# Output stores issued from SP instead of from ACT in a fused windowed-attention and feed-forward kernel

## The chip, the cores and the metric

The kernel runs on one core of one Trainium2 chip. The metric is the device time of one execution in microseconds (us); the time given is the median of 5 runs. A second source is one profiled execution, from which all durations below are read.

## The reference

For 8 batches of 8 heads with 576 positions of 64 values the kernel computes attention in a window of 32 positions to each side, puts the heads side by side into a matrix x of 4608 tokens by 512, and feeds it through two matrix products with a leaky ReLU between them:

```python
scores = q @ k.T / 8                      # per batch and head
scores = where(|i - j| <= 32, scores, -1e9)
attn   = softmax(scores)
x      = (attn @ v) as [B * S, H * D]     # 4608 x 512
h      = x @ w_in                         # 512 -> 2048
out    = maximum(0.01 * h, h) @ w_out     # 2048 -> 512
```

Inputs and output are float32; the kernel computes its products in bfloat16 with float32 sums.

## The kernel before

Work is staged in units that an outer program written by hand interleaves.

*Attention.* The heads are taken in 4 pairs a batch and the 576 queries in 2 halves, so there are 64 steps. Step i needs the score (`score`): five small matmuls into the PSUM tile `ps` (there is one such buffer), an exponential on ACT into `e` (L248), and on GpSimd (POOL) the product with the window mask into `pr` (L252). Then `weighted` has the row sums `s` (L274, or L276 and L279) and the weighted values `x` (L286) on PE, and a reciprocal (L292) and a product into `xT` (L294) on VectorE (DVE). Scores run one or two steps ahead of `weighted`.

*Inputs.* `load_qk` and `load_v` bring q, k and v of one batch and one pair into float32 tiles `qf`, `kf` and `vf` (L72 and L83; v in two halves). There is one buffer for each of the four pairs, so the load of the next batch can start only once the casts to bfloat16 have read the buffer: `cast_qk` (L168, on POOL, in the opening on DVE too) into `qb` and `kb`, and `cast_v` (L178) into `vbd`. q and k have to be transposed: for the first three batches PE does it (L201), from batch 3 on DMA transposes do (L187), issued once the cast is done. ACT copies the transposed q and k into `qT` and `kT` (L209, L215), and DVE places the keys into `kbd` (L227).

*Feed-forward.* `h_tile` computes one 128 x 288 tile of h (four matmuls, L305) and ACT applies the leaky ReLU (L309). `o_tile` computes 128 tokens of the output: 16 matmuls of 512 columns (L322), a copy from PSUM into `o_sb` by ACT (L327), and a store to the output in DRAM (L328). There are 36 such tiles; the last is cut into two parts of 384 and 128 columns, so there are 37 stores. `o_sb` has four buffers.

*Order.* Nothing is reordered by a scheduler; each engine works through its instructions in the order in which the program writes them. A list `plan` holds the h and o tiles, and `spend` (called before each h tile and, as the hook, four times inside each o tile) puts an attention step between them when its due time has come. So a step's casts, loads and DMA transposes are written in the middle of an o tile's matmuls, and a tile's store after them.

*Queues.* The engine SP issues all loads of q, k and v and all DMA transposes, and does nothing else. POOL issues the loads of the two weight matrices, all in the first 32 us. ACT issues the stores, between its activations. A DMA instruction waits in its engine's queue until its semaphores are there: for a store, the copy of its `o_sb`; for a load, the casts that read its buffer. Besides, in the built program the DMAs of SP and ACT together share eight completion counters, and each DMA waits until the previous one on its counter is done, whichever engine issued that.

Of the kernel before, what the change touches and what calls it, by code (L numbers as in the profile page):

```python
# [16 lines left out]
def kernel(  # L17
# [12 lines left out]
    nc = tc.nc  # L30
# [107 lines left out]
    for lo in (0, 64):  # L138
        w = win[lo:lo + 64]
        nc.gpsimd.affine_select(  # L140
            out=w, in_=w, compare_op=ALU.is_ge, fill=0.0,
# [3 lines left out]
            out=w, in_=w, compare_op=ALU.is_ge, fill=0.0,  # L145
# [167 lines left out]
    def o_tile(j, hook=None):  # L313


        cols = (0, 512) if j < NTOK // 128 - 1 else (0, 384, 512)
        for lo, hi in zip(cols[:-1], cols[1:]):
            o = mmps.tile([128, 512], FP32, name="mm", tag="mm")
            for f in range(FFC):
                if hook and lo == 0 and f % 4 == 0:  # L320
                    hook()
                nc.tensor.matmul(  # L322
                    o[:, lo:hi], gT[:, f, ds(128 * j % RING, 128)], w_out_bf[:, f, lo:hi],
                    start=(f == 0), stop=(f == FFC - 1),
                )
            o_sb = outp.tile([128, DMODEL], FP32, name="o_sb")
            nc.scalar.activation(out=o_sb[:, lo:hi], in_=o[:, lo:hi], func=AF.Copy)  # L327
            nc.scalar.dma_start(out=out[ts(j, 128), lo:hi], in_=o_sb[:, lo:hi])  # L328

    def keep_busy(n):  # L330

# [204 lines left out]
    for us, kind, g, f in plan:  # L536
        if kind == "h":
            spend(us)
            h_tile(g, f)
        elif f == 0:  # L540
            o_tile(g, lambda: spend(O_US))
# [28 lines left out]
```

## Time and profile before

| what | value |
|---|---|
| median of 5 runs | 328.82 us (327.81 to 329.25) |
| profiled execution: its own time | 328.82 us |
| profiled execution: span, first to last instruction | 327.1 us |
| PE busy | 306.7 us, 94% of the span |
| DVE, ACT, POOL busy | 226.3 us (69%), 223.3 us (68%), 180.5 us (55%) |
| SP's DMA queue q1 | 34.22 MB, packets' time 55.4% of 16 DMA engines |
| ACT's DMA queue q10 (the stores) | 9.44 MB, 8.3% |
| POOL's DMA queue q0 (the weights) | 4.20 MB, 7.7% |
| issue of one store on ACT | 0.34 us, 37 times |

How to read it: times on a timeline count from the start of the span. PE is the matmuls, PEld the weight loads beside them; ACT, DVE and POOL are the other compute engines; a q behind an engine's name (SPq, ACTq) marks an instruction by which its queue issues a DMA. Such an instruction does not count as busy, nor does waiting for a semaphore. In a list of waits each row says who waited for whom, the total in us, how often, and the longest. PEclk is the share of TensorE's full clock that was granted.

By stretches of the span PE is busy for 9.15 of the first 20 us, 17.32 of the next 20, 9.90 of the 10 to 50 us, 13.52 of the 16 to 66 us and 23.84 of the 24 to 90 us; from 90 to 306 us it is busy for 214.9 of 216 us. The first store is issued at 56.75 us, the last at 324.53 us.

### The profile page before, as it was taken

The numbers are of one execution on the slowest core, as the hardware profiler recorded it, in microseconds if no ns is written. First come the engines' busy times: TensorE is split into PE (matmuls) and PEld (weight loads), VectorE is DVE, ScalarE is ACT, GpSimd is POOL, SyncE is SP. The second block draws the span as 40 slices with busy tenths as digits, with TensorE's granted clock in tenths as the row PEclk, the third lists the DMA queues.
The fourth block names the chain that finished last, engine by engine and source line by source line (L and its number), as shares of the span: only waits on it lengthen the run. The fifth ranks groups of instructions, "written<-read, shape, count | busy, mean of one in ns | idle before, by whom it ended". The sixth has DMA issues, their size and how long they took to land.

```text
span 327.1 us, 6571 instructions
## 1 busy us (share of the span) xinstructions
PE 306.7 (94%) x2463; PEld 205.7 (63%) x2485; DVE 226.3 (69%) x310; ACT 223.3 (68%) x432; POOL 180.5 (55%) x213
## 2 busy tenths in 40 slices
PE   2578999799999999999999999999999999999996
PEld 1346784367585665757575766667675767676653
DVE  5489743579874997779777988688858867565200
ACT  5784792249385898878787888878786646465541
POOL 7699748647774696519741597339642545131000
PEclk9999999899999999999999999999999999999999
DMA  8999979968999999945995199916831001010102
GB/s 182 212 201 217 270 192 202 238 166 195 233 181 214 208 209 240 203 127 121 207 230 129 69 181 249 210 66 95 181 82 65 34 17 50 0 66 0 67 13 84
DMA packets 85172, 48.28 MB, mean 148 GB/s; under 512 B 64020, under 2 KB 80660, under 8 KB 85140
## 3 DMA queue, kind: packets, MB, share of 16 engines
q1 hardware_dynamic: 75524, 34.22, 55.4%
q10 hardware_dynamic: 5328, 9.44, 8.3%
q0 software_dynamic: 4288, 4.20, 7.7%
q8 instruction: 19, 0.31, 0.4%
q14 instruction: 13, 0.11, 0.1%
HBM read 36.70 MB, written 9.44 MB: 141 GB/s over the span
## 4 chain that ended last, share of the span: by engine, by line
PE 80%; DMA 9%; DVE 3%; SPq 3%; POOL 2%; issue 1%; ACT 0%; ACTq 0%; DVEq 0%
PE mm L322 35%; PE mm L305 34%; DMA kf<-in_k_dram 9%; PE ps L242 4%; PE x L286 4%; DVE r L292 2%; PE s L274 2%; SPq L72 2%; SPq L83 1%; POOL vbd L484 1%; PE tp L201 1%; DVE xT L294 1%; POOL kb L168 1%; POOL pr L252 1%; PE mm L335 0%
## 5 line engine op out<-in xcount | busy, mean ns | idle before, releaser
L292 DVE RECIPROCAL r<-s 128x288 f32<-128x288 f32 x64 | 125.1, 1954 | 34.5 <-PE s L274 25.1
L252 POOL TENSOR_TENSOR pr<-e,mask 128x544 bf16<-128x544 bf16 x64 | 78.0, 1218 | 101.8 <-ACT e L248 81.9
L305 PE MATMUL mm<-xT,w_in_bf 128*128 128x288 bf16 x1024 | 133.1, 286 | 0.0
L322 PE MATMUL mm<-w_out_bf,gT 128*128 128x512 bf16 (+2 forms) x571 | 129.9, 376 | 1.1
L309 ACT ACTIVATE gT<-mm 128x288 bf16<-128x288 f32 x256 | 101.0, 414 | 21.1 <-PE mm L305 8.6
L305 PEld LDWEIGHTS <-w_in_bf 128*128 128x128 bf16 x1024 | 98.3, 98 | 23.9
L322 PEld LDWEIGHTS <-gT 128*128 128x128 bf16 x592 | 56.8, 99 | 60.7 <-issue 1.7
L248 ACT ACTIVATE e<-ps 128x544 bf16<-128x544 f32 x64 | 40.0, 624 | 25.9 <-PE ps L242 6.0
L327 ACT ACTIVATE o_sb<-mm 128x512 f32<-128x512 f32 (+2 forms) x37 | 21.7, 586 | 47.0 <-PE mm L322 47.0
L227 DVE COPY kbd<-kT 64x576 bf16<-64x576 bf16 x64 | 28.6, 447 | 29.2 <-ACT kT L215 28.7
L178 POOL CAST vbd<-vf 64x576 bf16<-64x576 f32 x58 | 38.7, 668 | 2.2 <-DMA vf<-in_v_dram 0.3
L294 DVE TENSOR_TENSOR xT<-x,r 128x288 bf16<-128x288 f32 x64 | 29.3, 458 | 6.7
L168 POOL CAST kb<-kf 96x768 bf16<-96x768 f32 x32 | 27.4, 857 | 10.1 <-DMA kf<-in_k_dram 10.1
L242 PE MATMUL ps<-qT,kbd 128*128 128x128 bf16 (+2 forms) x320 | 26.8, 216 | 2.1 <-ACT e L248 2.1
L286 PE MATMUL x<-pr,vbd 128*128 128x128 bf16 (+2 forms) x320 | 26.4, 215 | 1.4 <-DVE xT L294 0.9
L242 PEld LDWEIGHTS <-kbd 128*128 128x128 bf16 x320 | 20.9, 101 | 10.6 <-issue 2.8
L263 DVE TENSOR_TENSOR both<-pr 128x256 bf16<-128x256 bf16 x52 | 23.0, 441 | 3.6 <-POOL pr L252 2.5
L209 ACT ACTIVATE qT<-qT 128x576 bf16<-128x576 bf16 x20 | 23.6, 1179 | 1.2 <-ACT o_sb L327 1.2
L286 PEld LDWEIGHTS <-vbd 128*128 128x128 bf16 x320 | 21.0, 99 | 4.9 <-issue 1.6
L215 ACT ACTIVATE kT<-kT 128x576 bf16<-128x576 bf16 x20 | 23.6, 1179 | 0.0
L265 DVE COPY both<-pr 128x32 bf16<-128x32 bf16 x52 | 21.7, 417 | 0.0
L168 POOL CAST qb<-qf 96x768 bf16<-96x768 f32 x24 | 19.7, 822 | 0.0
(39 smaller groups left out, 110.3 us busy)
## 6 DMA issues: line engine op xcount, KB each, us to landing
qf<-in_q_dram SPq DMA_DIRECT2D x32, 288.0 KB, 4.7
kf<-in_k_dram SPq DMA_DIRECT2D x32, 288.0 KB, 5.4
vf<-in_v_dram SPq DMA_DIRECT2D x64, 144.0 KB, 5.3
out_dram<-o_sb ACTq DMA_DIRECT2D x35, 256.0 KB, 2.1
w_in_bf<-in_moe_w_in_dram POOLq DMA_DIRECT2D x8, 256.0 KB, 6.8
w_out_bf<-in_moe_w_out_dram POOLq DMA_DIRECT2D x4, 512.0 KB, 14.0
qT<-qb SPq DMA_TRANSPOSE x20, 4.9
kT<-kb SPq DMA_TRANSPOSE x20, 4.0
```

The source lines that it names most:

```text
L168: eng.tensor_copy(out=dst[:, p], in_=src[b, p].rearrange("p a (c d) -> p c a d", d=D),)
L178: nc.gpsimd.tensor_copy(out=vbd[b % 2][r, p, :, r], in_=vf[b, p][r])
L227: nc.vector.tensor_copy(out=kbd[b % 2][r, p, :, r], in_=kT[r].rearrange("p (n j) -> p n j", j=64),)
L242: nc.tensor.matmul(ps[:, c0:c0 + n], kbd[b % 2][:, p, blk], qT[b][:, p, q0:q0 + n], start=True, stop=True,)
L248: nc.scalar.activation(out=e, in_=ps[:, 512 - HALF:512 - HALF + NCOL], func=AF.Exp, scale=scale,)
L252: nc.gpsimd.tensor_mul(pr, e, mask[hf])
L286: nc.tensor.matmul(x[:, a:a + n], vbd[b % 2][:, p, blk, :], pr[:, c0:c0 + n], start=(n_ == 0), stop=(n_ == len(WIN[hf]) - 1), skip_group_c ...
L292: nc.vector.reciprocal(r, s)
L294: nc.vector.tensor_mul(xT[:, p, t0:t0 + HALF], x, r)
L305: nc.tensor.matmul(h[:, 0:HALF], w_in_bf[:, c, ts(f, 128)], xT[:, c, ds(t0, HALF)], start=(c == 0), stop=(c == DMC - 1),)
L309: nc.scalar.activation(out=gT[:, f, ds(t0, HALF)], in_=h[:, 0:HALF], func=AF.Prelu, alpha=0.01,)
L322: nc.tensor.matmul(o[:, lo:hi], gT[:, f, ds(128 * j % RING, 128)], w_out_bf[:, f, lo:hi], start=(f == 0), stop=(f == FFC - 1),)
```

## The change

The store of `o_tile` is issued from SP (`nc.sync`) instead of from ACT (`nc.scalar`). Nothing else is edited:

```diff
             o_sb = outp.tile([128, DMODEL], FP32, name="o_sb")
             nc.scalar.activation(out=o_sb[:, lo:hi], in_=o[:, lo:hi], func=AF.Copy)
-            nc.scalar.dma_start(out=out[ts(j, 128), lo:hi], in_=o_sb[:, lo:hi])
+            nc.sync.dma_start(out=out[ts(j, 128), lo:hi], in_=o_sb[:, lo:hi])
```

In the built program PE, DVE and POOL keep their instructions and their order. ACT loses the 37 stores. SP gets them at the places where the program writes them: the first before the load of `qf` of batch 2 and pair 0, the second before `qf` of pair 1, and so on; those from 248 us on come after all loads and transposes. Which of the eight counters a DMA uses changes with this for nearly all DMAs after the first store.

## The prediction

> **What bounds the kernel now.** I read the page first (busy shares, then the chain that ended last), then the waits of PE and of ACT, then the stretch from 50 to 70 us in small windows and as a timeline. PE is busy for 94% of the span and holds 80% of the chain, so the question is where PE loses time at all. The list of PE's waits for the whole span has one entry of size once the opening is over, and ACT's list has its cause:
>
> ```profile
> PE ps L242 <- ACT e L248: 2.1, 1, 2.1
> ...
> ACT e L248 <- DMA vf<-in_v_dram: 4.0, 1, 4.0
> ACT e L248 <- DMA kf<-in_k_dram: 3.6, 1, 3.6
> ```
>
> The columns are total us, times, longest. An exponential reads PSUM and needs no DMA, yet ACT sat before two of them until a load landed. From 70 us to the end PE's waits sum to only 0.3 us. The chain, in order of time (start, us, what), shows what stood between:
>
> ```profile
> 54.52 6.91 DMA kf<-in_k_dram
> ...
> 61.50 0.34 ACTq L328
> ...
> 61.94 0.64 ACT e L248
> ...
> 62.62 0.40 PE ps L242 x5
> ```
>
> The second output store stood in ACT's queue until that load landed, although its data was ready at 57.74 + 0.59 = 58.33. In the built program each DMA of SP or ACT counts on one of eight completion counters and waits until that counter's previous DMA is done; the second store got the counter of this kf load (issued 54.52), the first store that of the last vf load before it (issued about 51.0). The timeline of ACT has both holds:
>
> ```profile
> 57.22 0.62 ACT L248 ACTIVATE e<-ps 128x544 bf16<-128x544 f32 x1 [4.04 <-DMA vf<-in_v_dram]
> ...
> 61.94 0.62 ACT L248 ACTIVATE e<-ps 128x544 bf16<-128x544 f32 x1 [3.60 <-DMA kf<-in_k_dram]
> ```
>
> PE pays twice, as windows of 2 us show (length, then PE busy; PEclk is the number ahead of the last two):
>
> ```profile
> 60.00:62.00 2.00, 0.54 (x3) 0.14 (x2) 1.03 (x2) 0.06 (x1) 0.54 (x1) 1.00 1.15 227
> 62.00:64.00 2.00, 1.38 (x14) 1.06 (x14) 0.71 (x1) 1.19 (x2) 1.29 (x2) 0.80 1.13 234
> 64.00:66.00 2.00, 2.00 (x7) 0.60 (x6) 1.70 (x2) 0.60 (x1) 1.86 (x3) 0.50 1.13 247
> ```
>
> First it is idle for 2.1 us, then it runs at half clock. PE's timeline prices the second part:
>
> ```profile
> 63.43 3.46 PE L322 MATMUL mm<-w_out_bf,gT 128*128 128x512 bf16 x8
> ```
>
> The next score matmul starts at 66.73, so eight of these took 3.30 us where the full pace (16 in 3.45 us on the chain, for example from 141.64) is 0.216 us each, 1.73 us.
>
> [...]
>
> **The change part by part.**
> (a) Removed from ACT: 37 issues of 0.34 us, 12.6 us, with their counter waits. From 70 us on this is worth nothing on the path: PE waits 0.3 us there and ACT has room (58.8 of 72 us busy in 162 to 234). The cover is PE's own work, and ACT stays shorter than PE.
> (b) Removed: the two holds. Without the first, ACT does the score of 57.22 about 3.5 us earlier; without the second, that of 61.94 can follow its matmuls (58.34) at once. PE's wait goes: **-2.0 us** (2.1 less a usual hop). With no such hole the half clock goes too: 3.30 - 1.73 = **-1.6 us**. What could be late next is POOL's mask product, the DVE chain, or a vbd cast: POOL is busy 10.6 of 16 us in 52 to 68, so 3.6 us less leaves it 10.6 of 12.4. I allow **+0.2 us** for a new small gap there (today's wait of x for a cast is 0.4).
> (c) Added to SP: the same 37 issues, 12.6 us, each waiting for its o_sb from ACT. SP has room on average (it stands 48.3 us at L187 waiting for POOL's kb), but it takes turns, so I went through its new order. In 53 to 66 us the first store comes just before the load of qf of batch 2; its data is there at 52.59 + 0.60 = 53.2, so that load goes 0.5 us late. The second comes before qf1, kf1, qf2 and kf2 (now 54.02 to 55.50) and its data comes only near 57.9 (nine of its sixteen matmuls run from 55.35 on at 0.216 us, then the copy of 0.59): those four go 3.9 us late, the vf halves behind them 4 to 5 us, qf3 and kf3 (59.03, 60.20) 5 to 6 us. In these is that the first vf half now waits for the first store's counter (53.3 plus a landing of 7.4, so 60.7). Who waits: the batch 2 casts. kf3, the tightest, lands near 60.20 + 7.9 = 68.1 (7.9 is the kf median from issue to landing in 50 to 70 us) and is first read by POOL at 82.77, 14.7 us later; less 6 us for the delay and 3.5 us for the earlier reader, 5 us remain. Cost 0, covered by that slack. After 100 us, stores stand ahead of DMA transposes: stores issued now at 106.79, 110.85, 145.76, 183.52, 217.82, 234.97, transposes behind them at 109.95, 114.21, 148.91, 186.66, 220.96, 238.73. The store is ready 3.1 to 3.8 us before the transpose may start, since that waits for a POOL cast: cost 0.
> (d) The other way round, stores wait behind SP's loads and transposes (a transpose issues in 1.2 us and more). With four o_sb buffers and a store every 3.4 to 13 us a store may be some 10 us late before ACT waits for a buffer: cost 0, and it has no effect below nothing.
> (e) Stores and loads on one ring. The bytes are the same; q10's share is 8.3% of 16 engines. Nearest row: a store lands in 7.4 us among loads, 2.1 us in quiet. Bounds: from 0.5 us gained[...] to 5 us lost (rival 3). I take 0.
> (f) The tail: the last store needs a hop from ACT to SP, as the gaps of 0.05 to 0.1 us between SP's instructions suggest: +0.1 us. ACT no longer issues (0.34) between the last two copies, but the second waits for PE, so nothing comes back.
> Sum: -2.0 - 1.6 + 0.2 + 0.1 = **-3.3 us**. The profiled execution took 328.82 us (span 327.1 plus 1.7), which is also the median of the runs shown, so 325.5.
>
> **Rivals.** (1) *The gain is halved by POOL.* POOL is full from 50.3 to 56.5 (memsets, two products, four casts), and its products feed PE. If it is late by 1.5 to 2 us in place of ACT and PE's clock still drops for a while: 327.2. For it: with 10.6 us of work in 12.4 us POOL has little room. Against: from 56.5 POOL waits for ACT 1.50 us and then 2.17 us.
> (2) *Nothing moves.* The holds on ACT return as holds of the loads, and PE waits for loads instead: 328.8. Against: the slack of 5 us in (c), and that the two stores' new counters belong to vf loads issued near 47 and 48 us.
> (3) *Slower: the shared ring makes transposes late.* Four keys are near their use: kT issued at 187.98, 193.52, 222.27 and 226.54, with the median landing of 4.0 us, are read by ACT (L215) at 193.91, 198.66, 228.20 and 232.97, so 1.1 to 2.4 us spare. If landings on the one ring grew by 4 us, batch 6 would lose 4 - 1.1 = 2.9 and batch 7 4 - 1.9 = 2.1 us, 5 us in all: 330.5. It decides from about 3.2 us of growth, where the two overruns reach 3.3. Against: stores near those transposes are issued 3 us earlier and land in about 2 us. The extreme is a tenth of that chance, some 335.
>
> **How the numbers follow.** Forecast (-3.3, with 324.5 to 326.6 for its own spread: 1 us for the clock, 0.5 for a run): 0.72. Rival 1: 0.11. Rival 2: 0.06. Rival 3: 0.11. The bound of what a measurement tells from no change is 0.3%, 1 us. Faster is forecast and most of rival 1: 0.82; within it rival 2 and a rest: 0.07; slower rival 3: 0.11. The range goes from 324.0 to 327.9: it leaves out rival 3, part of rival 2 and little below.
>
> **What would show it.** Right: the two DMA entries are gone from ACT's waits; 60 to 66 us has PE full and PEclk 1.00; SP shows L328, with the qf and kf loads behind the second store near 58 us; PE's waits after 70 us stay under 1 us; span near 323.8. Wrong in (b): PEclk still falls near 60 us, or PE waits for POOL. Wrong in (c): POOL's or DVE's casts of batch 2 wait for DMA near 70 to 85 us. Wrong in (e): ACT waits at L209 or L215 for a DMA and PE waits after 100 us.

## The result and the profile after

The changed kernel takes 327.42 us (median of 28 runs, 326.05 to 328.61) where the kernel before takes 328.63 us (median of 49). The ratio is 0.9961, with a 95% interval of 0.9950 to 0.9973: 1.2 us faster, where 3.3 us were forecast.

The part near 60 us went as forecast. The page's PEclk row shows nines throughout; windows of 2 us (length, PE busy, ..., PEclk third from the end) of the profile after show it in place:

```profile
60.00:62.00 2.00, 1.85 (x15) 0.95 (x13) 2.00 (x2) 0.89 (x2) 1.86 (x3) 1.00 1.06 253
62.00:64.00 2.00, 2.00 (x20) 1.23 (x19) 1.90 (x5) 0.95 (x2) 0.70 (x2) 1.00 1.14 237
64.00:66.00 2.00, 1.95 (x14) 1.05 (x14) 1.77 (x4) 0.08 (x1) 0.81 (x1) 1.00 1.26 231
```

PE is busy 5.8 of these 6 us at full clock (before: 3.9, much of it at half). (Among PE's busy times given ahead of the prediction, 9.90 us belong to 40 to 50 us, 13.52 us to 50 to 66 us and 23.84 us to 66 to 90 us.) ACT's waits in 50 to 66 us name no DMA any more:

```profile
ACT o_sb L327 <- PE mm L322: 7.3, 4, 2.4
ACT e L248 <- PE ps L242: 3.8, 3, 1.8
ACT e L248 <- POOL vbd L178: 0.6, 1, 0.6
```

SP's timeline (start, length, instruction) shows the new order, with the four loads of q and k held by the second store until 57.15:

```profile
53.04 0.58 SPq L328 DMA_DIRECT2D out_dram<-o_sb  x1
53.72 0.37 SPq L72 DMA_DIRECT2D qf<-in_q_dram  x1
54.19 0.42 SPq L72 DMA_DIRECT2D kf<-in_k_dram  x1
57.15 0.36 SPq L328 DMA_DIRECT2D out_dram<-o_sb  x1
57.60 0.39 SPq L72 DMA_DIRECT2D qf<-in_q_dram  x1
```

What was not forecast stands in PE's waits from 70 us to the end, which summed to 0.3 us before:

```profile
PE s L274 <- DVE r L292: 1.0, 1, 1.0
PE x L286 <- DVE xT L294: 0.6, 2, 0.3
```

A good yardstick is the start of ACT's copy of an output tile (L327), because a tile's copy follows PE's progress. From tile to tile, in us, with the medians of the two kernels:

| kernel | median | start to tile 0 | tile 0 to 4 | 4 to 11 | 11 to the last copy | last copy to end |
|---|---|---|---|---|---|---|
| before | 328.63 | 52.59 | 31.94 | 56.55 | 183.14 | 2.90 |
| after | 327.42 | 52.05 | 28.17 | 58.32 | 183.12 | 3.40 |
| difference | -1.2 | -0.54 | -3.77 | +1.77 | -0.02 | +0.50 |

The first column is chance: no instruction differs there, and it ran from 52.05 to 54.38 us over the profiles of this study. Without it the profiles differ by 1.5 us, about what the medians do. So 3.8 us were gained, and 1.8 us were given back between tiles 4 and 11 and 0.5 us at the end.

Where the 1.8 us went: of the profile before, the timelines of DVE and of POOL near 125 us.

```profile
125.28 0.29 DVE L263 TENSOR_TENSOR both<-pr 128x256 bf16<-128x256 bf16 x1
125.49 0.17 DVE L265 COPY both<-pr 128x32 bf16<-128x32 bf16 x1
125.57 1.95 DVE L292 RECIPROCAL r<-s 128x288 f32<-128x288 f32 x1
```
```profile
126.03 1.22 POOL L252 TENSOR_TENSOR pr<-e,mask 128x544 bf16<-128x544 bf16 x1 [1.47 <-issue]
```

The same two, and PE, of the profile after, at the same step (24, the first of batch 3):

```profile
120.97 0.29 DVE L263 TENSOR_TENSOR both<-pr 128x256 bf16<-128x256 bf16 x1
121.18 1.19 DVE L265 COPY both<-pr 128x32 bf16<-128x32 bf16 x1
122.29 1.95 DVE L292 RECIPROCAL r<-s 128x288 f32<-128x288 f32 x1
```
```profile
121.12 1.22 POOL L252 TENSOR_TENSOR pr<-e,mask 128x544 bf16<-128x544 bf16 x1 [1.47 <-issue]
```
```profile
124.29 0.28 PE L274 MATMUL s<-both,ones_bd 128*128 128x288 bf16 x1 [1.03 <-DVE r L292]
```

DVE copies 32 columns. Before, it was through 0.4 us ahead of POOL's product; after, the product starts 0.06 us ahead of the copy, and the copy ends 0.03 us after the product does, so it takes 1.19 us. The reciprocal behind it is 1 us late, and PE, which needs the single buffer `s` back, waits 1.03 us. The next step collides too, there with POOL's casts of q and k:

```profile
125.64 0.79 DVE L263 TENSOR_TENSOR both<-pr 128x256 bf16<-128x256 bf16 x1
126.35 0.80 DVE L265 COPY both<-pr 128x32 bf16<-128x32 bf16 x1
```
```profile
125.46 0.82 POOL L168 CAST qb<-qf 96x768 bf16<-96x768 f32 x1
126.23 0.89 POOL L168 CAST kb<-kf 96x768 bf16<-96x768 f32 x1
```

Why they meet now: ACT's timeline after the copy of tile 9, before and after.

```profile
124.18 0.61 ACT L327 ACTIVATE o_sb<-mm 128x512 f32<-128x512 f32 x1
124.82 0.34 ACTq L328 DMA_DIRECT2D out_dram<-o_sb  x1
125.27 0.62 ACT L248 ACTIVATE e<-ps 128x544 bf16<-128x544 f32 x1 [0.48 <-ACT o_sb L327]
```
```profile
119.89 0.59 ACT L327 ACTIVATE o_sb<-mm 128x512 f32<-128x512 f32 x1
120.37 0.62 ACT L248 ACTIVATE e<-ps 128x544 bf16<-128x544 f32 x1
```

The exponential followed the copy's start by 1.09 us and now follows it by 0.48 us, so POOL's product comes 0.6 us sooner after it. DVE's copy does not (1.31 and 1.29 us after the start of ACT's copy). The store issue on ACT had been keeping the two apart.

### The profile page after: what moved, and what is told of

Read it like the earlier page. It is cut to its first block, busy times and chain, and to the rows that moved or that the text cites. A ratio compares the mean times of both kernels' runs of the same rounds, so it can differ in the third digit from the quotient of the medians.

```text
span 325.1 us, 6587 instructions
## 1 busy us (share of the span) xinstructions
PE 305.2 (94%) x2463; PEld 205.2 (63%) x2485; DVE 224.6 (69%) x310; ACT 224.7 (69%) x432; POOL 180.3 (55%) x213
## 3 DMA queue, kind: packets, MB, share of 16 engines
q1 hardware_dynamic: 80852, 43.66, 63.6%
## 4 chain that ended last, share of the span: by engine, by line
PE 77%; DMA 7%; DVE 6%; POOL 3%; SPq 2%; ACT 2%; issue 2%; DVEq 0%; POOLq 0%; ACTq 0%
PE mm L322 34%; PE mm L305 32%; DMA kf<-in_k_dram 7%; PE x L286 4%; PE ps L242 4%; DVE r L292 4%; PE s L274 2%; SPq L72 1%; SPq L83 1%; POOL vbd L484 1%; DVE xT L294 1%; PE tp L201 1%; POOL kb L168 1%; ACT kT L215 1%; POOL vbd L178 1%
## 5 line engine op out<-in xcount | busy, mean ns | idle before, releaser
L322 PE MATMUL mm<-w_out_bf,gT 128*128 128x512 bf16 (+2 forms) x571 | 128.3, 373 | 1.1
L309 ACT ACTIVATE gT<-mm 128x288 bf16<-128x288 f32 x256 | 104.4, 413 | 25.2 <-PE mm L305 9.6
L327 ACT ACTIVATE o_sb<-mm 128x512 f32<-128x512 f32 (+2 forms) x37 | 21.7, 586 | 55.8 <-PE mm L322 55.8
L227 DVE COPY kbd<-kT 64x576 bf16<-64x576 bf16 x64 | 28.5, 446 | 24.8 <-ACT kT L215 24.2
L265 DVE COPY both<-pr 128x32 bf16<-128x32 bf16 x52 | 22.7, 437 | 0.0
L263 DVE TENSOR_TENSOR both<-pr 128x256 bf16<-128x256 bf16 x52 | 21.2, 408 | 0.5
```

The source lines that it names most:

```text
L227: nc.vector.tensor_copy(out=kbd[b % 2][r, p, :, r], in_=kT[r].rearrange("p (n j) -> p n j", j=64),)
L309: nc.scalar.activation(out=gT[:, f, ds(t0, HALF)], in_=h[:, 0:HALF], func=AF.Prelu, alpha=0.01,)
L322: nc.tensor.matmul(o[:, lo:hi], gT[:, f, ds(128 * j % RING, 128)], w_out_bf[:, f, lo:hi], start=(f == 0), stop=(f == FFC - 1),)
```

## The experiments

Theory A is this collision. Theory B is that the moved stores make loads or transposes late on SP or in its queue q1, where the page of the profile after has the stores too (43.66 MB, no q10; the prediction and an expectation call that queue a ring). Kernels of one group share the runs of the kernel before. Ratios are to that kernel, with the 95% interval.

**First group** (before: 328.92 us).

All stores from SP, the changed kernel again.

> The changed kernel again, beside its variants. Theory A (a collision gives the gain back): PE gains 3.5 to 4 us between 50 and 66 us; near 121 us the DVE copy L265 runs while POOL's product L252 runs and takes 1.2 us in place of 0.17, PE waits for the reciprocal about 1 us there and 1.5 us in all, and about 0.5 us goes at the end; so 1.2 to 2 us faster than before. Theory B (the moved stores make transposes or loads late): the same total, but ACT or POOL wait for a DMA after 100 us.

327.89 us, ratio 0.9965 (0.9950 to 0.9981). Its profile repeats the pattern: 28.08 us from tile 0 to 4, 58.31 us from 4 to 11, 3.40 us at the end. No wait of ACT or PE for a DMA appears after 100 us. POOL's list there puts two waits of its mask product, 3.8 us in all, down to a DMA; in the kernel before it has four, 6.8 us in all, so Theory B's sign is absent.

The first four stores alone from SP:

```diff
-            nc.sync.dma_start(out=out[ts(j, 128), lo:hi], in_=o_sb[:, lo:hi])
+            (nc.sync if j < 4 else nc.scalar).dma_start(out=out[ts(j, 128), lo:hi], in_=o_sb[:, lo:hi])
```

> The stores of tiles 0 to 3 from SP, all others from ACT as before. Theory A: the holds at 53 to 61 us are gone, ACT keeps its 0.34 us issue near 120 us so POOL's product comes after the DVE copies, and the tail is that of before: 3.3 to 3.8 us faster than before, 325.0 +- 0.5. Theory B would also give this, since no store stands among transposes. If the gain near 60 us is itself smaller than 3.5 us, this one shows only 1 to 2 us.

325.37 us, ratio 0.9909 (0.9876 to 0.9943), so 3.6 us faster. 28.33, 56.55 and 2.91 us in the same three places: the gain is kept and nothing is given back. The forecast's size was right for this part.

All from SP but tile 9 (`j != 9`):

> All stores from SP except that of tile 9 (the copy at about 119.9 us), which ACT issues. Theory A: the exponential behind it comes about 0.45 us later, POOL's product starts after the DVE copies, L265 near 121 us takes 0.17 us, and 1.2 to 1.7 us come back against all_sp (about 326). Theory B: one store in 37 changes nothing on a ring, so the same time as all_sp within 0.3 us.

326.39 us, ratio 0.9918 (0.9892 to 0.9944). Against all_sp 1.5 us come back in the medians (0.5 of them at the end, which takes 2.91 us here). Between tiles 4 and 11 it takes 57.34 us, 1.0 us less than all_sp and 0.8 us more than before. L265 of step 24 is down to 0.17 us, and one collision is left, in the next step, as DVE's timeline shows:

```profile
126.29 1.19 DVE L265 COPY both<-pr 128x32 bf16<-128x32 bf16 x1
```

All from SP, step 24 not joined:

```diff
-        if JOINED - 1 <= i < NC - 1:
+        if JOINED - 1 <= i < NC - 1 and i + 1 != 24:
```

> All stores from SP; step 24 alone is not joined: its two DVE instructions L263 and L265 are gone and PE makes the row sums from the two parts of pr with two matmuls (L276, L279; 0.1 us more), the result being the same sum. Theory A: the collision near 121 us has no DVE copy to hit, PE's wait for the reciprocal goes, 1.0 to 1.6 us come back against all_sp. Theory B: no change, within 0.3 us.

326.85 us, ratio 0.9938 (0.9914 to 0.9962), 1.0 us better than all_sp by the medians; the two intervals overlap a little, so the profile has to carry this. Its stretch from tile 4 to 11 takes 57.56 us, 0.8 us less than all_sp. Here too the collision moved on by one step, and PE's waits still have it:

```profile
PE s L274 <- DVE r L292: 0.7, 1, 0.7
```

Theory B expected no change from either kernel; in the profiles one store alone moves 1.0 us of this stretch, and one join alone 0.8 us.

**Second group** (before: 328.64 us).

The kernel before, with tiles 9 and 10 alone from SP (`j in (9, 10)`):

> The kernel before, with the stores of tiles 9 and 10 alone moved to SP. Theory A (freeing ACT of the 0.34 us issue in that place lets POOL's product meet the DVE copies): slower than before, by 1.0 to 1.8 us, about 330.3; L265 near 125.5 us takes 1.2 us and PE waits for the reciprocal there, while the hole at 60 us and the half clock stay. Theory B (what was lost is a matter of SP's queue as a whole): two stores more on SP change nothing, within 0.3 us of before.

330.75 us, ratio 1.0067 (1.0041 to 1.0093): slower by 2.1 us, with the interval from 1.3 to 3.1. The stretch from tile 4 to 11 takes 58.31 us, as in all_sp: two of the 37 stores carry its whole loss. DVE's and POOL's timelines:

```profile
125.49 1.21 DVE L265 COPY both<-pr 128x32 bf16<-128x32 bf16 x1
```
```profile
125.45 1.22 POOL L252 TENSOR_TENSOR pr<-e,mask 128x544 bf16<-128x544 bf16 x1 [0.88 <-POOL vbd L178]
```

and PE's waits, the old hole of 60 us (`ps`) among them:

```profile
PE s L274 <- DVE r L292: 1.8, 2, 1.0
PE ps L242 <- ACT e L248: 1.7, 1, 1.7
PE x L286 <- DVE xT L294: 1.0, 4, 0.3
```

Of these, one wait for the reciprocal (1.0 us) and two for `xT` (0.6 us) are near 128 to 134 us. The others belong to the hole, and there an expectation missed: the half clock did not stay. PEclk is 1.00 throughout, and PE's timeline has the same eight matmuls at full pace, but then a wait that the profile before does not have:

```profile
62.58 0.40 PE L242 MATMUL ps<-qT,kbd 128*128 128x64 bf16 x5 [1.74 <-ACT e L248]
63.29 1.89 PE L322 MATMUL mm<-w_out_bf,gT 128*128 128x512 bf16 x8
69.83 0.28 PE L274 MATMUL s<-both,ones_bd 128*128 128x288 bf16 x1 [0.78 <-DVE r L292]
```

From tile 0 to 4 it takes 31.35 us, hardly less than the 31.94 us before.

The kernel before, with tile 1 alone from SP (`j == 1`):

> The kernel before, with the second store alone (tile 1, the one that stood for the kf load until 61.50 us) moved to SP. If that hold alone made PE's hole and the half clock: all of first4_sp's gain, 3.3 to 3.8 us, about 325.4, with ACT still held near 57 us. If the first hold matters as much: about half.

324.98 us, ratio 0.9898 (0.9867 to 0.9929), 3.7 us faster: one store has the whole gain. One expectation missed: ACT is not held near 57 us by the first store either, which it issues at once, as its timeline shows.

```profile
53.51 0.38 ACTq L328 DMA_DIRECT2D out_dram<-o_sb  x1
54.91 0.62 ACT L248 ACTIVATE e<-ps 128x544 bf16<-128x544 f32 x1 [1.43 <-PE ps L242]
```

Moving the second store changed the counters of its neighbours too. So this kernel takes away both holds, and the weight of each alone isn't settled by it.

All from SP but tiles 9 and 10 (`j not in (9, 10)`):

> All stores from SP except tiles 9 and 10, which ACT issues. Theory A: j9_act had one collision left (L265 of the next step, 1.19 us at 126.3 us, with 0.8 us of PE lost); with the second store on ACT too, L265 takes 0.17 us in both steps and 0.5 to 0.9 us more come back: 325.6 to 326.0, within 0.5 us of first4_sp. Theory B: as all_sp, near 327.8.

324.85 us, ratio 0.9888 (0.9863 to 0.9913), the fastest by its median, 3.8 us faster than before and 0.8 us below the expected range. The stretch takes 56.56 us, 0.8 us less than j9_act, as expected; the medians differ by 1.5 us, more than the profiles explain. In step 24 the copy is through before the product starts, in DVE's and POOL's timelines:

```profile
122.07 0.17 DVE L265 COPY both<-pr 128x32 bf16<-128x32 bf16 x1
```
```profile
122.84 1.21 POOL L252 TENSOR_TENSOR pr<-e,mask 128x544 bf16<-128x544 bf16 x1 [2.29 <-issue]
```

With 35 of 37 stores on SP, Theory B has nothing left to explain.

All from SP but the last two tiles (SP for `j < 34`; with the last tile's two parts these are three stores, not the four of the expectation):

> All stores from SP except the last four (tiles 34 and 35), which ACT issues: 0.3 to 0.5 us faster than all_sp if the longer time from the last copy to the end of the span (3.1 us in all_sp's profile, 2.6 in first4_sp's) belongs to SP's issue; no difference if it is a matter of chance in the landing. The collisions near 121 us stay, so about 327.4 at best.

326.96 us, ratio 0.9955 (0.9933 to 0.9976), against 0.9965 for all_sp: the intervals overlap, so the times are inconclusive. In the profile the end takes 2.92 us in place of 3.40 (the expectation counts it from the end of the last copy, the table from its start).

**Third group** (before: 328.92 us).

All from SP, steps 24 and 25 not joined (`i + 1 not in (24, 25)`):

> All stores from SP, steps 24 and 25 not joined (the DVE instructions L263 and L265 of both are gone, PE makes the row sums from the two parts of pr: 0.1 us more a step, the same sum). Theory A (collisions of DVE copies with POOL's product): with no copy left to hit in the two steps, the time from tile 4's to tile 11's copy is back at 56.6 to 56.9 us (58.3 with the collisions), and the kernel is 2.7 to 3.5 us faster than before. If the issue on ACT mattered in another way than through the collision, the 58.3 us stay.

325.51 us, ratio 0.9898 (0.9866 to 0.9930), 3.4 us faster; the stretch takes 56.38 us. ACT is as free as in the changed kernel, POOL's products come as early, and with no DVE copy to hit in these steps the loss is gone. By itself this edit also takes 0.46 us of undisturbed DVE work from each of the two steps; but j9_10_act keeps both joins, undisturbed, and its stretch is as short (56.56 us). Together they show that it was the collision, not the freed ACT in another way.

Tiles 0 to 3 from ACT, the others from SP (`j >= 4`):

> The counterpart of first4_sp: tiles 0 to 3 stored from ACT, all others from SP. If the change is the sum of two parts (a gain of some 3.6 us in the first four stores, a loss of some 2.1 us in tiles 9 and 10 and 0 to 0.5 us at the end), this is 1.8 to 2.6 us slower than before, about 331.

330.40 us, ratio 1.0049 (1.0034 to 1.0063): slower by 1.5 us, a little less than expected. 31.42 and 58.32 us: almost no gain, the full loss of 1.8 us, but an end of 2.92 us. Here too the hole is there (1.49 us) and PEclk stays at 1.00. The end's 0.5 us that I had counted as part of the loss isn't there.

## Why the prediction fell short, step by step

**Reading what bounds the kernel** was right: ACT's holds made PE's hole, and after the opening no other loss of PE of that size was there to be had. That the half clock follows from the hole was an estimate from one profile, and does not hold for the others (see (b)).

**(b), the holds:** right in its sum, with 3.6 us less 0.2 forecast and 3.77 us measured, but partly by luck. The half clock was priced at 1.6 us on top of the hole. In the profiles of only9_10_sp and rest_sp the hole is there without it, and tile 0 to 4 still takes 31.35 and 31.42 us, 3.2 to 3.3 us more than in the changed kernel: its matmuls run at full pace, and PE then waits 0.8 us for a reciprocal and 0.4 us for `xT`. So the hole with what follows it costs 3.2 us or so at full clock, and the half clock only 0.5 to 0.6 us more. The runs of the kernel before in the three groups agree: 46 of 75 had a mean clock of 0.998 or more (the profiled one, with 3.4 us at half, has 0.995) and a median of 328.57 us, the other 29 one of 329.20 us. In the profile before, PE was busy for 1.95 of the 2 us from 58 to 60, then idle for 2.08 us at a stretch, and the drop came after that (PEclk 0.50 in 64 to 66 us). The idle stretches of 1.74 us in only9_10_sp and of 1.49 us in rest_sp were followed by none. How long an idle stretch has to be, and whether its length alone decides, these three profiles do not show.

POOL, feared as the next to be late, kept up (PE's one wait in 48 to 70 us of the profile after is 0.2 us, for `xT`), so rival 1's mechanism did not come in that stretch. That its number, 327.2, is close to the time measured is chance.

**(c), SP's new order:** right. The second store was issued at 57.15 (57.9 forecast) and the four loads behind it at 57.60 to 59.10; no cast of batch 2 waited for DMA, and the transposes were not late. Rival 2 falls with it.

**(d), (e), stores and loads in one queue:** right at 0. In the profile after, the stores' bytes are in SP's queue (q1 has 43.66 MB, and there is no q10). A store landed in 2.2 us (2.1 before), qf and kf in 4.4 and 5.2 us (4.7 and 5.4), transposes in 4.4 and 3.6 us (4.9 and 4.0). Rival 3 asked for transposes 3 us later; it did not come.

**(a), ACT's freed issue, is the step that failed.** It said that from 70 us on this "is worth nothing on the path", because PE hides ACT there. It cost 1.8 us, through a chain that the step did not follow: a faster ACT gives POOL its product sooner, the product now starts ahead of a DVE copy and holds it (1.19 us in place of 0.17), and PE's only buffer for the row sums comes back late. PE's waits after 70 us, which were to stay under 1 us, came to 1.6 us. The sum used busy shares and PE's waits of before; both say how much room there is on average, not which instructions will now run at once. I had asked what is late next only in 50 to 68 us, where time was gained, not wherever an issue was removed. The material was in the profile before: the page gives L265 a mean of 417 ns, while by itself it takes 0.16 to 0.17 us. Of the 52 copies, the 26 that overlap no work of POOL took 0.161 to 0.170 us, and 20 of the other 26 took 0.64 to 1.19 us. That an overlap with POOL costs a DVE copy time, and how much, is read from these durations; what the two engines contend for, they do not tell.

**(f), the end:** forecast at +0.1, measured at +0.5 us. The traces place it: the last store lands 2.42 us after the start of the last copy, 1.92 us before the change. SP issues it 0.1 us later, as forecast; the rest is its landing. Why it lands later stays open. It is not simply SP's issue: with the last stores on SP the end took 2.91 to 2.92 us in three kernels (j9_act, j9_10_act, rest_sp) and 3.3 to 3.4 us in four, where that store lands at 2.28 to 2.42 us (1.92 or 1.93 us in all others). The four are those in which ACT issues no store at all. Why that should matter wasn't tried.

So: -3.8 + 1.8 + 0.5 = -1.5 us by the profiles, -1.2 us by the medians.

## What to carry to other kernels

Moving a DMA to another engine's queue moves its waits too: look at what a store or load waits for (here a completion counter last used by a load: the second store's data was ready at 58.33 us, that load landed at 61.43, and the store was issued at 61.50), because moving one store was worth 3.7 us, and moving two others cost 2.1 us. Removing a small piece of work shifts what stands behind it, also where nothing was idle (0.34 us of issue gone from ACT, POOL's product 0.6 us sooner, PE 1.0 us late); for each engine that gets faster, ask which instructions of others it will now overlap, and read the spread of an instruction's durations, not its mean, to see what an overlap costs. A slow clock seen in one profile need not be there in other executions (46 of 75 of the kernel before had a mean clock of 0.998 or more): look at the clock of the other runs before pricing it. A change made at many places can be split by place: moving one store, or all but two, gained three times what moving all did.

## What the runs showed of the hardware that was not expected

A DVE copy of 128 x 32 bf16 (L265) takes 0.16 to 0.17 us alone and up to 1.21 us beside a POOL product of 1.22 us, seven times as long. It looks held rather than slowed: in the twelve profiles 243 of these copies began 0.04 to 0.20 us after a POOL instruction, and every one ended 0.03 or 0.04 us after that instruction, whether it was a product of two tensors or a cast of one (0.79 us beside a cast of q or k, 0.65 us beside one of v). The 301 additions of 128 x 256 bf16 (L263, 0.28 to 0.29 us alone) that began after a POOL instruction ended 0.14 to 0.21 us after it, with up to 0.92 us beside a cast and 1.35 us beside a product. The one that starts first is spared: 37 additions and 8 copies that began up to 0.26 us ahead of a product kept their usual time. So did the nine copies of the profiles before and after that began 0.006 to 0.013 us behind a cast of v (0.16 us).

Not every DVE instruction is held. In the profiles before and after, the reciprocal, which reads PSUM, kept its 1.94 to 1.96 us beside the same POOL instructions, and the copies of the keys (L227, 64 x 576 bf16) their 0.43 to 0.45 us.
